# Six attention steps moved between the groups of the bias, the first two units in plain fp32 scores, a lag of four steps

## The chip, the cores and the metric

One core of a Trainium2 chip runs the whole program. The metric is the device time of one execution in microseconds (us). TensorE (PE) multiplies, VectorE (DVE), ScalarE (ACT) and GpSimd (POOL) work on tiles, and SyncE (SP) issues nearly all DMAs. PEld is the loading of weights into TensorE.

## The reference

Relative-position attention, whose output is the input of a three-way max MoE. B = 4, H = 8, S = 576, D = 64:

```python
scores = (q @ k.T) / sqrt(D)
psi = log1p(|i - j|) / log1p(max(i, 1))
bias = relu(psi[..., None] @ w1 + b1) @ w2          # (S, S, H), the same for every batch
attn = softmax(scores + bias)
x = (attn @ v) -> (2304, 512)
h = max(x @ m_w1, x @ m_w2, x @ m_w3)               # 512 -> 768
out = h @ m_w_out                                   # 768 -> 512
```

## The kernel before

The program has three stages.

**The bias** (`bias_stage`, L89). The 576 rows i are cut into 36 groups of 16. In iteration i the loop makes `hidden` of one group (four tiles `hid`, 128 x 304 to 576, by relu: three on DVE at L108 and one on ACT at L111, as a running balance `load` of the two engines decides), `product` of the group before (plain fp32 matmuls with `w2s` into a PSUM tile `bp`, L129) and `finish` of the one before that (`bp` scaled into `bs`, on ACT at L149 or on DVE at L152, and written by an SP DMA to `bias_d` in DRAM, L156). The groups 32 to 35 come first (`todo`, L132), since the small last row tile t = 4 (64 rows, `biasm`) needs them. `load_bias` (L162) reads the bias of one row tile t of a head pair back from `bias_d`, once all of its groups are written: the full tiles t = 0 to 3 are 576 KB each.

**Attention** (`Attention`, L182). There are 16 units (head pair, batch) of five row tiles t, 80 steps. A step n has a front end and a back end. In the front, `front` makes the scores `s` of both heads (one combined head for t = 4) as three fp32r products of high and low halves (L235, L244; the halves are made by `prep`, a cast on ACT at L212 and a subtraction on POOL at L213), `shift` adds the bias and takes the row minimum on DVE (L254), `expo` takes the exponential and its sum on ACT (L266, L270), and one step later `norm` takes the reciprocal on DVE (L276) and multiplies `e` by it on POOL (L279). In the back, LAG = 5 steps later, `flip` transposes `e` on PE into `tp` and `lp` (L298, L307) and ACT and DVE copy them to `et` (L389, L390, L392). Every 2 or 3 row tiles, five pairs of fp32 matmuls `pv` (L337) are queued; each step pops one to three of them. `split_x` (L345) splits the finished `pv` into `xhi` and `xlo`. The first five steps have no back end and run small `warm` matmuls on PE (L314).

**The MoE** (`moe`, L443): fp32r products of `xhi`, `xlo` with the weights' halves.

Every engine runs its instructions in the order of the program text; the order is written out by hand. PSUM tiles: `s` and `tp` have two buffers each, `lp` and `pv` one. In the bias stage `bp` takes all eight banks with four buffers; that pool is released before the attention's pool is opened (L542), so the first `s` comes after the last `bs`. `load_qk` brings the raw q and k of a unit (two buffers), `load_v` its v.

## Time and profile before

| | |
|---|---|
| median of 3 runs | 610.79 us (610.71 to 610.86) |
| profiled execution, span | 610.0 us |
| bias stage, first `hid` to the end of the last `bs` | 4.7 to 49.8 us |
| first matmul of the MoE | 310.7 us |
| PE busy | 600.2 us, 98% of the span |
| DVE, ACT, POOL busy | 368.1, 296.7, 171.0 us |

The profile is of one execution. A busy PE is not PE at its peak, since a matmul's end is modelled and a waiting one can look busy; so progress is read from the starts of steps, not from the busy share. In rows of the timeline that merge instructions, the time of one instruction is worked out from the start of the group and the start of what follows it.

### The profile page before, as it was taken

What the parts mean: (1) busy time and instruction counts of PE and PEld (TensorE: products, weight loads), DVE (VectorE), ACT (ScalarE), POOL (GpSimd) and SP (SyncE); (2) the same over time, 40 slices, a digit from 0 to 9 for tenths busy, and PEclk for the clock granted to TensorE, in tenths of its full rate; (3) what the DMA queues carried; (4) which work ended last, traced back from release to release, by engine and by line L of the source; (5) the groups of instructions that cost most, each with busy time, mean ns of one, the idle gap of its engine ahead of it and who ended that gap; (6) DMA issues with size and microseconds to landing.
All of it is one profiled execution on the core that took longest, in us unless ns stands there. A gap on an engine that the chain in (4) does not pass through costs nothing.

```text
span 610.0 us, 11550 instructions
## 1 busy us (share of the span) xinstructions
PE 600.2 (98%) x4288; PEld 464.0 (76%) x4288; DVE 368.1 (60%) x942; ACT 296.7 (49%) x791; POOL 171.0 (28%) x189
## 2 busy tenths in 40 slices
PE   8998899999999999999999999999999999999997
PEld 4456667776667767676678989889898898988886
DVE  7995776677777777776544746646464562233231
ACT  7997888888888888887510000000010001134432
POOL 2704766656676675574300000000000000000000
PEclk9999999999999999999999999999999999999999
DMA  5897435522462255200211212212122110011111
GB/s 170 245 332 257 144 93 144 156 72 70 148 172 61 62 165 163 62 16 18 55 35 35 70 34 70 69 35 72 40 65 66 40 64 1 1 53 70 52 70 69
DMA packets 48007, 55.16 MB, mean 90 GB/s; under 512 B 21968, under 2 KB 31568, under 8 KB 47952
## 3 DMA queue, kind: packets, MB, share of 16 engines
q1 hardware_dynamic: 47808, 54.14, 29.0%
q8 instruction: 34, 0.56, 0.4%
q10 hardware_dynamic: 144, 0.29, 0.2%
q14 instruction: 21, 0.17, 0.1%
HBM read 38.81 MB, written 15.61 MB: 89 GB/s over the span
## 4 chain that ended last, share of the span: by engine, by line
PE 90%; ACT 5%; DMA 2%; issue 2%; DVE 1%; SPq 0%; DVEq 0%
PE pv L337 14%; PE tp L298 12%; PE s L244 12%; PE h L483 8%; PE h L485 8%; PE h L484 8%; PE g L485 4%; PE g L483 4%; PE g L484 4%; PE o L508 4%; PE o L507 4%; PE o L509 4%; ACT bs L149 2%; ACT hid L111 2%; DMA bias<-bias_d 1%
## 5 line engine op out<-in xcount | busy, mean ns | idle before, releaser
L266 ACT ACTIVATE e<-sn,nm 128x576 f32<-128x576 f32 x144 | 110.9, 772 | 44.5 <-DVE nm L254 40.7
L279 POOL TENSOR_SCALAR e<-e,rc 128x576 f32<-128x576 f32 x144 | 105.8, 748 | 69.2 <-DVE rc L276 23.1
L254 DVE CUSTOM_DVE_ANT_0 sn<-s,bias 128x576 f32<-128x576 f32 x128 | 91.7, 754 | 42.6 <-PE s L244 36.8
L490 ACT COPY m<-h 128x512 f32<-128x512 f32 (+1 forms) x30 | 16.3, 544 | 206.2 <-PE h L485 180.9
L483 PE MATMUL h<-xhi,wh 128*128 128x512 f32 (+1 forms) x240 | 88.3, 368 | 0.0
L485 PE MATMUL h<-xhi,wl 128*128 128x512 f32 (+1 forms) x240 | 88.3, 368 | 0.0
L484 PE MATMUL h<-xlo,wh 128*128 128x512 f32 (+1 forms) x240 | 88.2, 368 | 0.0
L298 PEld LDWEIGHTS tp<-ident,e 128*128 128x128 f32 x576 | 61.5, 141 | 34.6 <-issue 29.4
L298 PE MATMUL tp<-ident,e 128*128 128x128 f32 x576 | 80.8, 280 | 0.9 <-ACT et L389 0.8
L337 PE MATMUL pv<-et,vt 128*64 128x256 f32 (+1 forms) x496 | 73.6, 417 | 0.0
L392 DVE COPY et<-tp 128x512 f32<-128x512 f32 x64 | 43.9, 686 | 26.3 <-PE tp L298 25.8
L244 PE MATMUL s<-kh,qh 64*128 64x288 f32 (+1 forms) x288 | 57.2, 343 | 2.3 <-DVE nm L254 1.4
L462 DVE TENSOR_TENSOR hl<-ht,hh 128x128 fp32r<-128x128 f32 x108 | 23.4, 286 | 44.9 <-ACT hh L461 44.9
L491 DVE TENSOR_TENSOR m<-h,m 128x512 f32<-128x512 f32 (+1 forms) x30 | 19.1, 638 | 50.9 <-ACT m L490 50.4
L483 PEld LDWEIGHTS h<-xhi,wh 128*128 128x128 f32 x240 | 45.1, 188 | 6.2 <-issue 0.5
L213 POOL TENSOR_TENSOR kl<-kr,kh 128x640 fp32r<-128x640 f32 x16 | 35.6, 2223 | 50.2 <-ACT kh L212 50.2
L484 PEld LDWEIGHTS h<-xlo,wh 128*128 128x128 f32 x240 | 45.0, 188 | 5.7
L485 PEld LDWEIGHTS h<-xhi,wl 128*128 128x128 f32 x240 | 45.0, 188 | 5.7
L389 ACT COPY et<-tp 128x512 f32<-128x512 f32 x80 | 45.8, 573 | 6.9 <-PE tp L298 6.9
L244 PE MATMUL s<-kl,qh 64*128 64x288 f32 (+1 forms) x288 | 48.6, 293 | 0.0
L244 PE MATMUL s<-kh,ql 64*128 64x288 f32 (+1 forms) x288 | 48.0, 290 | 0.0
L337 PEld LDWEIGHTS pv<-et,vt 128*64 128x64 f32 x496 | 30.3, 136 | 22.2 <-issue 9.8
(85 smaller groups left out, 1060.7 us busy)
## 6 DMA issues: line engine op xcount, KB each, us to landing
bias_d<-bs SPq DMA_DIRECT2D x36, 295.5 KB, 6.1
bias<-bias_d SPq DMA_DIRECT2D x16, 576.0 KB, 4.0
w<-in_moe_w_dram SPq DMA_DIRECT2D x18, 512.0 KB, 3.5
qr<-in_qd_dram SPq DMA_DIRECT2D x16, 320.0 KB, 3.2
kr<-in_kd_dram SPq DMA_DIRECT2D x16, 320.0 KB, 4.0
out_dram<-ot SPq DMA_DIRECT2D x17, 256.0 KB, 2.0
vt<-in_v_dram SPq DMA_DIRECT2D x32, 128.0 KB, 2.7
w64o<-in_moe_w_out_dram SPq DMA_DIRECT2D x6, 512.0 KB, 3.2
```

Source lines behind the costliest of these rows:

```text
L213: nc.gpsimd.tensor_tensor(out=lo, in0=r, in1=hi.bitcast(F32), op=ALU.subtract)
L244: nc.tensor.matmul(ss[h][:, x, 0:HALF], lhsT=u[q][p, r], rhs=u[k][p, c:c + HALF], start=(j == 0), stop=(j == 2))
L254: nc.vector.tensor_tensor_reduce(out=sn.rearrange("p (a b) -> p a b", a=2), in0=st["s"][h][:, :, 0:HALF], in1=bt.rearrange("p (a b) -> p a ...
L266: nc.scalar.activation(st["e"][:, S * h:S * h + S], sn, ACTF.Exp, scale=-1.0, bias=nm, accum_out=st["sm"][:, h:h + 1])
L279: nc.gpsimd.tensor_scalar(out=e, in0=e, scalar1=rc[:, h:h + 1], scalar2=1.0, op0=ALU.mult, op1=ALU.mult)
L298: nc.tensor.transpose(tp[:, 128 * c:128 * c + 128], e2[:, k0:k0 + 128], ident)
L337: nc.tensor.matmul(pv[p], lhsT=w, rhs=x, start=(c == 0), stop=(c == NTQ))
L389: nc.scalar.copy(*tps[0])
L392: nc.vector.tensor_copy(*tps[1])
L483: nc.tensor.matmul(o, lhsT=hi[:, r], rhs=x, start=(c == 0), stop=False)
L484: nc.tensor.matmul(o, lhsT=hi[:, r], rhs=y, start=False, stop=False)
L485: nc.tensor.matmul(o, lhsT=lo[:, r], rhs=x, start=False, stop=(c == KDM - 1))
```

## The change

- The scores `s` get a PSUM pool of their own that lives through the program; the bias products keep two `bp` buffers instead of four.
- Units 0 and 1 are never split by `prep`: their scores are one plain fp32 product of the raw q and k (L235). Their four casts on ACT and four subtractions on POOL go away.
- The fronts of units 0 and 1 run tile by tile (t = 4, 0, 1, 2, 3, each for unit 0 and unit 1). Six of these ten steps (t = 4, 0, 1) run in the bias stage: `front` in the iterations 12, 13, 21, 23, 29, 31, `shift` one iteration later, `expo` two and `norm` four iterations later. The balance `load` counts 770 ns a head for the shift on DVE and 970 ns a head for the exponential on ACT.
- The loads of the bias move: t = 4 from iteration 12 to 9, t = 0, 1, 2 from 19, 27, 35 to 17, 25, 33. Raw q and k get three buffers and come in iterations 0, 2 and 20, v of units 0 and 1 in iteration 14.
- After the bias stage the steps follow a written plan: the back ends start at once, four steps behind the fronts instead of five; two steps have no front; the `warm` matmuls are gone.

```diff
@@ -47,8 +47,10 @@
+    psum_s = ctx.enter_context(tc.tile_pool(name="psum_s", bufs=1, space=PSUM))
+
     def ps_s(name):
-        return psums[-1].tile([128, 2, 512], F32, tag="s", bufs=2, name=name)
+        return psum_s.tile([128, 2, 512], F32, tag="s", bufs=2, name=name)
...
-            bp = psums[-1].tile([128, 1024], F32, tag="bp", bufs=4, name=f"bp{g}")
+            bp = psums[-1].tile([128, 1024], F32, tag="bp", bufs=2, name=f"bp{g}")
...
+        nf = dict(zip(FIRST, range(len(FIRST))))
         for i in range(NG + 2):
             if i < NG:
                 hidden(todo[i])
             if 0 < i <= NG:
                 product(todo[i - 1])
+            if i in nf:
+                at.front(nf[i])
+            if i - 1 in nf:
+                n = nf[i - 1]
+                for h in range(at.heads(n)):
+                    at.shift(n, h)
+                    load["dve"] += 770
             if i > 1:
                 x = todo[i - 2]
                 finish(pool, k, load, x, late.pop(x))
+            if i - 2 in nf:
+                n = nf[i - 2]
+                for h in range(at.heads(n)):
+                    at.expo(n, h)
+                    load["act"] += 970
+            if i - 4 in nf:
+                at.norm(nf[i - 4])
...
-    sched = [(un, t) for un in range(len(units)) for t in range(NS)]
-
-    fronts = [sched[x] for x in (0, 1, 2, 4, 5, 3)] + sched[6:]
+    HEAD = [(un, t) for t in (4, 0, 1, 2, 3) for un in (0, 1)]
+    fronts = HEAD + [(un, t) for un in range(2, len(units)) for t in range(NS)]
+    sched = [(0, 0), (0, 1), (1, 0), (1, 1), (0, 2), (0, 4), (1, 2), (0, 3), (1, 4), (1, 3)]
+    sched = sched + fronts[len(HEAD):]
     NSTEP = len(sched)
-    LAG = NS
+    FIRST = (12, 13, 21, 23, 29, 31)
...
-            kr = pool.tile([128, S + LEFT], F32, tag="kr", bufs=2, name=f"kr{un}")
-            qr = pool.tile([128, S + LEFT], F32, tag="qr", bufs=2, name=f"qr{un}")
+            kr = pool.tile([128, S + LEFT], F32, tag="kr", bufs=3, name=f"kr{un}")
+            qr = pool.tile([128, S + LEFT], F32, tag="qr", bufs=3, name=f"qr{un}")
...
-            terms = (("qh", "kh"), ("qh", "kl"), ("ql", "kh"))
+            terms = (("qr", "kr"),) if "qr" in u else (("qh", "kh"), ("qh", "kl"), ("ql", "kh"))
...
-                st["e"] = pool.tile([128, 2 * S], F32, tag="e", bufs=NS + 2, name=f"e{n}")
+                nh = self.heads(n)
+                st["e"] = pool.tile([128, nh * S], F32, tag=f"e{nh}", bufs=7 if nh > 1 else 2, name=f"e{n}")
...
-        def warm(self, n):
-            w = psums[-1].tile([128, 128], F32, tag="l", bufs=1, name=f"warm{n}")
-            for _ in range(4):
-                nc.tensor.matmul(w, lhsT=ident, rhs=ident, start=True, stop=True)
...
-        def step(self, n, more=None):
-            m, f = n - 1, n - LAG
+        def step(self, n, f, pops, more=None):
             nh = 0
-            if n < NSTEP:
+            if n is not None:
                 un, t = fronts[n]
                 hp, b = units[un]
-                if t == 0 and un and un + 2 < len(units):
+                if t == 0 and 2 <= un < len(units) - 2:
                     self.load_qk(un + 2)
-                if t == 3 and un:
-                    self.load_v(un)
                 nh = self.heads(n)
                 self.front(n)
-            if n < NS:
-                self.warm(n)
-            for _ in range((1, 3, 2, 2, 2)[n % NS]):
-                if self.pvq and n >= LAG + TS + 1:
+                if (un, t) == HEAD[-1]:
+                    self.load_qk(3)
+            for _ in range(pops):
+                if self.pvq:
                     self.pvq.pop(0)()
-            back = 0 <= f < NSTEP
+            if n is not None and t == 4 and un > 1:
+                self.load_v(un)
...
+            for m in self.raw:
                 self.norm(m)
-            if n < NSTEP and un + 1 < len(units):
-                t0 = 1 if un == 1 else 0
+            self.raw = [] if n is None else [n]
+            if n is None:
+                un, t = (1, f - 2)
+            if 1 <= un < len(units) - 1 and (n is None or un > 1) and f < NSTEP:
...
+        def run(self, more):
+            lag = 4
+            first = len(FIRST)
+            plan = [(first, 0, 0), (first + 1, 1, 0), (None, 2, 2), (None, 3, 3), (first + 2, 4, 3), (first + 3, 5, 2)]
+            early = {6: 0, 7: 0, 8: 2, 9: 2, 10: 1}
+            for f in range(6, NSTEP):
+                n = f + lag if f + lag < NSTEP else None
+                plan.append((n, f, early.get(f, (3, 2, 2, 2, 1)[(f - 1) % NS])))
+            for n, f, pops in plan:
+                self.step(n, f, pops, more if f >= NSTEP - 60 and (n is None or n % NS >= 2) else None)
+            while self.pvq:
+                self.pvq.pop(0)()
+            self.split_x()
...
-            for g, _ in enumerate(bias_stage(bp)):
+            for g, _ in enumerate(bias_stage(bp, at)):
                 if g == 0:
                     at.load_qk(0)
+                if g == 2:
+                    at.load_qk(1)
+                if g == 9:
+                    load_bias(0, NTQ)
+                if g in (17, 25, 33):
+                    load_bias(0, (g - 17) // 8)
+                if g == 14:
                     at.load_v(0)
-                    first = at.prep(0)
-                if g in (5, 8):
-                    next(first)
-                if g == 16:
-                    at.load_qk(1)
-
-                if g == 12:
-                    load_bias(0, NTQ)
-                if g in (19, 27, 35):
-                    load_bias(0, (g - 19) // 8)
+                    at.load_v(1)
+                if g == 20:
+                    at.load_qk(2)
             load_bias(0, NTQ - 1)
-            at.load_qk(2)
...
-        while n < NSTEP + LAG:
-            at.step(n, w0 if n >= NSTEP - 60 and n % NS >= 2 else None)
-            n += 1
-        while at.pvq:
-            at.pvq.pop(0)()
-        at.split_x()
+        at.run(w0)
```

## Rows read from the trace of the kernel before

**Rows 1.** The page, busy time and share of the span of PE:
```profile
PE 600.2 (98%) x4288; PEld 464.0 (76%) x4288; DVE 368.1 (60%) x942; ACT 296.7 (49%) x791; POOL 171.0 (28%) x189
```

**Rows 2.** Stretches: length, busy us of each engine, granted PE clock, DMA share, GB/s:
```profile
40.00:50.00 10.00, 8.84 (x130) 4.23 (x121) 8.51 (x22) 8.79 (x15) 0.00 (x0) 1.00 1.01 349
50.00:60.00 10.00, 9.19 (x78) 7.72 (x80) 5.42 (x17) 7.02 (x18) 5.55 (x6) 1.00 0.66 209
60.00:70.00 10.00, 8.75 (x78) 6.69 (x75) 6.80 (x20) 7.78 (x22) 5.77 (x9) 1.00 0.69 217
100.00:110.00 10.00, 10.00 (x87) 6.96 (x86) 6.87 (x20) 7.11 (x21) 5.91 (x7) 1.00 0.75 208
```

**Rows 3.** Timeline of DVE and ACT in the bias stage: start, us, instruction, [idle before]:
```profile
4.71 18.93 DVE L108 TENSOR_SCALAR hid<-sm,bp 128x528 f32<-128x528 f32 x48
...
32.47 6.66 DVE L108 TENSOR_SCALAR hid<-sm,bp 128x304 f32<-128x304 f32 x21
...
47.96 0.83 DVE L152 TENSOR_SCALAR bs<-bp,sm 128x591 f32<-128x591 f32 x1 [0.28 <-issue]
...
49.09 0.75 ACT L149 ACTIVATE bs<-bp,sm 128x591 f32<-128x591 f32 x1 [1.06 <-PE bp L129]
```

**Rows 4.** Groups by line, 0 to 50 us: busy, mean ns | idle before, releaser:
```profile
L152 DVE TENSOR_SCALAR bs<-bp,sm 128x591 f32<-128x591 f32 x4 | 3.3, 827 | 0.5 <-issue 0.3 <-ACT hid L111 0.2
...
L149 ACT ACTIVATE bs<-bp,sm 128x591 f32<-128x591 f32 x32 | 24.4, 761 | 2.9 <-PE bp L129 2.9
```

**Rows 5.** Timeline of one step's shift (DVE), exponentials (ACT), copies of a back end (ACT):
```profile
51.09 0.76 DVE L254 CUSTOM_DVE_ANT_0 sn<-s,bias 128x576 f32<-128x576 f32 x1 [2.30 <-DMA bias_d<-bs]
...
52.46 0.08 DVE L254 DVE_READ_ACCUMULATOR2_ANT nm<- 128x1 f32 x1
...
51.90 0.78 ACT L266 ACTIVATE e<-sn,nm 128x576 f32<-128x576 f32 x1 [2.06 <-DVE nm L254]
...
53.67 0.71 ACT L212 CAST kh<-kr 128x640 fp32r<-128x640 f32 x1
...
128.10 0.58 ACT L389 COPY et<-tp 128x512 f32<-128x512 f32 x1
...
128.73 0.78 ACT L266 ACTIVATE e<-sn,nm 128x576 f32<-128x576 f32 x1
```

**Rows 6.** Chain that ended last, PE's pieces: start, us, what:
```profile
27.38 5.25 PE bp L129 x80
...
118.09 0.99 PE s L244 x12
119.08 1.01 PE pv L337 x8
120.10 1.02 PE tp L298 x8
...
133.78 0.98 PE s L244 x9
```

**Rows 7.** POOL beside DVE: timeline of POOL, then DVE's groups by form:
```profile
12.77 12.29 POOL L213 TENSOR_TENSOR kl<-kr,kh 128x640 fp32r<-128x640 f32 x1 [10.71 <-ACT kh L212]
25.02 1.66 POOL L213 TENSOR_TENSOR ql<-qr,qh 128x640 fp32r<-128x640 f32 x1
...
129.80 1.48 POOL L279 TENSOR_SCALAR e<-e,rc 128x576 f32<-128x576 f32 x2
...
L108 DVE TENSOR_SCALAR hid<-sm,bp 128x384 f32<-128x384 f32 x6 | 3.7, 666 | 0.0
...
L108 DVE TENSOR_SCALAR hid<-sm,bp 128x400 f32<-128x400 f32 x6 | 2.2, 422 | 0.0
```

**Rows 8.** DMA issues at 22.6, 31.3 and 58.5 us: KB, us to landing:
```profile
biasm<-bias_d SPq DMA_DIRECT2D x1, 144.0 KB, 3.4
...
bias<-bias_d SPq DMA_DIRECT2D x1, 576.0 KB, 7.8
...
bias<-bias_d SPq DMA_DIRECT2D x1, 576.0 KB, 5.3
```

**Rows 9.** Timeline of PE: front of step n = 8, first matmul of the MoE:
```profile
71.00 0.40 PE L244 MATMUL s<-kh,qh 64*128 64x288 f32 x2
...
310.70 0.50 PE L483 MATMUL h<-xhi,wh 128*128 128x512 f32 x1
```

More of the change, by code (lines that the diff above doesn't have):

```diff
@@ L186, in __init__ @@
             self.st = {}
-            self.et = {}
+            self.ets = {}
+            self.left = {}
+            self.raw = []
             self.pvq = []
@@ L244, in front @@
                         nc.tensor.matmul(ss[h][:, x, 0:HALF], lhsT=u[q][p, r], rhs=u[k][p, c:c + HALF],
-                                         start=(j == 0), stop=(j == 2))
+                                         start=(j == 0), stop=(j == len(terms) - 1))
             self.st[n] = dict(s=ss)
@@ L286, in flip @@
             w = 128 * TS if g == 0 else S - 128 * TS
-            if t in (0, TS):
+            if (un, g) not in self.ets:
                 et = pool.tile([128, (2 * NTQ + 1) * (S - 128 * TS)], F32, tag="et", bufs=2, name=f"et{un}_{g}")
-                self.et = (et[:, 0:2 * NTQ * w].rearrange("p (c h q) -> p c h q", c=NTQ, h=2),
-                           et[:, 2 * NTQ * w:(2 * NTQ + 1) * w])
-            ea, el = self.et
+                self.ets[un, g] = (et[:, 0:2 * NTQ * w].rearrange("p (c h q) -> p c h q", c=NTQ, h=2),
+                                   et[:, 2 * NTQ * w:(2 * NTQ + 1) * w])
+                self.left[un, g] = TS if g == 0 else NS - TS
+            ea, el = self.ets[un, g]
             c0 = 128 * t - 128 * TS * g
@@ L340, in pair @@
                 return run
-            self.wait = True
             self.pvq.extend(pair(c) for c in range(NTQ + 1))
@@ L375, in step @@
                 next(more, None)
-            if n < NSTEP and b == B - 1 and hp + 1 < HP:
+            if n is not None and b == B - 1 and hp + 1 < HP:
                 load_bias(hp + 1, t)
-            if 0 <= m < NSTEP:
+            for m in self.raw:
                 self.norm(m)
-            if n < NSTEP and un + 1 < len(units):
-                t0 = 1 if un == 1 else 0
+            self.raw = [] if n is None else [n]
+            if n is None:
+                un, t = (1, f - 2)
+            if 1 <= un < len(units) - 1 and (n is None or un > 1) and f < NSTEP:
+                t0 = 1 if un == 2 else 0
                 if t == t0:
@@ L386, in step @@
             self.split_x()
-            if back:
+            if f is not None:
                 tps, left = self.flip(f)
@@ L392, in step @@
                     nc.vector.tensor_copy(*tps[1])
-            if back:
                 un, t = sched[f]
@@ L396, in step @@
                 w = 128 * TS if g == 0 else S - 128 * TS
-                if t in (TS - 1, NS - 1):
-                    self.queue_pv(un, 128 * TS * g, w, *self.et)
+                self.left[un, g] -= 1
+                if self.left[un, g] == 0:
+                    self.queue_pv(un, 128 * TS * g, w, *self.ets[un, g])
+        def run(self, more):
[11 more added lines that the diff above has]
+            self.split_x()
     def convert(pool, src, hi, lo, name, split=None):
```

5 lines of the change are left out of this document (2 added, 3 removed).

## The prediction, made before the changed kernel was run

> **What bounds the kernel now.** I read the page first: PE is busy 98% of the span [rows 1], which only says that most of the program is PE's. So I looked for the stretches where it is not, with the stretches by engine [rows 2]. From 100 us on PE is full and a unit takes 133.78 - 118.09 = 15.7 us, start to start [rows 6]; nothing there can be gained but PE work. The bias stage is another matter: DVE and ACT are nearly full, DMA is saturated at its end [rows 2], and the timeline shows DVE going from 4.71 to 48.79 with almost no gap [rows 3], 0.5 us of idle time in all against 2.9 us on ACT [rows 4]. DVE bounds that stage, ACT closely behind; its last `bs` ends at 49.84. Then comes a refill, 50 to 71 us: steps without back ends, bias loads that are waited for, two engines half used [rows 2]. From the front of step 8 at 71.00 PE runs without a break to the MoE at 310.70, 239.7 us later [rows 9].
>
> So the change pays through the refill: between 49.84 and 71.00 the old kernel does 8 fronts and 3 back ends, some 12 us of PE work in 21 us. It is paid for in the bias stage, on DVE, which has nothing to spare. The whole question is the size of that bill.
>
> **The bias stage, part by part.** Start: 44.08 us of DVE from 4.71 to 48.79.
>
> Taken away. The casts of unit 0 leave ACT and its two subtractions leave POOL. The latter matter: the first sat on POOL from 12.77 for 12.29 us, and while both were finishing, DVE's 384-wide `hid` slowed: six average 666 ns where the 400-wide take 422 [rows 7]. At 0.41 each these six should take 2.5 us and took 4.0, so DVE lost 1.5. With that and the 0.5 of idle time gone, 42.1 us of DVE work remain.
>
> Added. A two-head shift takes 52.46 - 51.09 + 0.08 = 1.45, a single one 0.76 [rows 5]: 4 x 1.45 + 2 x 0.76 = 7.3. Six reciprocals have no row here; at the size of the accumulator's read, 0.08 [rows 5], 0.5. The running balance, worked out by its formulas, gives DVE 4 `bs` before (as the trace shows [rows 4]) and 4 after, and moves four `hid` from ACT to DVE: at 0.32 to 0.39 (6.66/21 and 18.93/48 [rows 3]) 1.4. DVE: 42.1 + 7.3 + 0.5 + 1.4 = 51.3, from 4.7 to 56.0. The last `bs` waits for the last product, 1.05 us of PE (5.25 for five groups [rows 6]) with one `bs` between: 0.4, so 56.4 without any other wait.
>
> ACT gets 4 x 1.77 [rows 5] and 2 x about 1.05 for the exponentials, loses 1.2 of casts and 2.1 of `hid`: 42.2 busy becomes 48.1, done by about 53. It stays behind DVE. PE has 36 x 1.05 + some 6.5 for the fronts, 44 in 52 us: room enough, and two `bp` buffers suffice, since a product needs only the `bs` two groups before it.
>
> Waits that are new, each in DVE's queue with the `hid` of the next groups behind it, and through them PE and ACT:
> - t = 4: three loads issued after iteration 9's write land 3.4 us after issue [rows 8], some 5 us after that `bs`; DVE's four iterations take 4.5. Wait 0.4.
> - t = 0: behind iteration 17's write (0.6 to issue) the 576 KB take 5.3 in a calm queue and 7.8 in a saturated one [rows 8]; the v loads and the slower groups leave the queue calmer than before, so 5.3. DVE reaches the shift after 15 `hid` of 0.31, 4.8 us. Wait 1.1, at 7.8 it would be 3.6.
> - t = 1 has seven iterations' worth of time: 0.2.
> - Each front is emitted an iteration ahead of its shift: product and front, 1.05 + 1.1, against two iterations' `hid`, 2.1. Nothing.
> - POOL now multiplies ten heads by reciprocals here, 0.74 each [rows 7]. The row at 12.77 says that POOL waits out an unbroken run of `hid` and gets in when DVE does something else; the shifts, the DVE `bs` and the wait for t = 0 are such places and hold all but about one of the ten. I take 0.7; the ends are 0 and 7.4.
>
> Here the Trainium skill speaks against the change (SBUF — State Buffer, "Who interferes with whom"): a DVE `tensor_scalar` in a two-port mode and a GpSimd instruction share one port pair, and whichever issues first holds it for its whole duration while the other blocks. The slow `hid` agree with it. By that rule alone all ten multiplications could hold DVE up, and the stage would end 6.7 us later than in my sum.
>
> Sum: 56.4 + 0.4 + 1.1 + 0.2 + 0.7 = 58.8, 9.0 later than before. That is B.
>
> **The refill.** Plain fp32 scores: no row shows them. Nearest are plain fp32 `pv` pairs, 1.01 for two pairs of 256 columns, so 1.13 for two of 288; the fp32r front takes 0.99 [rows 6]. If the two heads did not run together on PE's row halves, 2.3. The fp32r heads do, and fp32 column halves do: 1.13.
>
> The first front of the plan runs on PE before B. Its shift starts at about B + 0.2 (bias t = 2, loaded four iterations earlier), its exponentials 0.8 later, and take 1.77; the copies of the first back end 0.63 [rows 5]: B + 3.4. The second front waits for the `s` buffers till B + 1.7, ends at 2.8, its exponentials begin at 3.7, end at 5.4; copies to B + 6.1. Only then can the first `pv` run. ACT bounds these 6.1 us, PE stands about half of them.
>
> From there compare with the old step 8. Still to do are the same 72 fronts and 160 `pv` pops, one more transposed step (1.02 and 0.1 for `lp` [rows 6]) and 0.25 for two plain fronts: 1.4. The steps five to eight back ends on have few or no pops: PE has 2.1 us, ACT 1.77 + 0.63 and a cast of 0.6 in two of them. Followed through, PE loses 0.4, 0.6 and 1.2 there: 2.2. The t = 3 bias lands by B + 11 (write, then 5.3), its front's successor needs it at B + 12: nothing. After that the lag of four is enough: with two heads the copies of a step end 4.4 to 5 us after its front starts, and the next transposes come at 5 or later, so the unit stays at 15.7.
>
> MoE start: 58.8 + 6.1 + 1.4 + 2.2 + 239.7 = 308.2 instead of 310.7. The MoE is untouched. Span 610.0 - 2.5 = 607.5; the median stands 0.8 above the profiled span, so **608.3 us**. The granted clock is 1.00 throughout [rows 2], its 2.4 GHz level; the `warm` matmuls fill waits and cost nothing. PE's longest new wait is under 2 us; no row here shows the lower level, so its price has no bound and sits in the tail.
>
> **The rivals.**
> 1. **DVE isn't held up and the refill is dense.** For: neither the waits (2.4) nor the 2.2 of ACT-bound steps has a row; against: the copies follow the exponentials on ACT by the program's order. 608.3 - 4.6 = 603.7. Chance 0.18.
> 2. **POOL holds DVE.** The multiplications start in the gap of a reciprocal and each stops the next `hid`. For: 1.5 us lost to two POOL instructions [rows 7]; against: the first of these waited 11 us without harm. Each head exposed beyond the one counted costs 0.74; from five on (3.7) the kernel is slower than before by over 0.2%; eight give 608.3 + 5.9 = 614.2, six 612.7. I take **612.7**. Chance 0.16.
> 3. **The bias loads come late.** At 7.8 instead of 5.3 the wait for t = 0 grows by 2.5: 610.8, no change. For: DMA share 1.01 before [rows 2]; against: the qk loads no longer fall there. Chance 0.16.
> 4. **Plain fp32 scores cost double**, so that the change doesn't do what it says: 1.1 more for each of four fronts in the bias stage, where shifts wait for them, and four behind it: 608.3 + 8.8 = 617.1. Chance 0.05.
>
> **How the numbers follow.** The forecast (its own range 606.3 to 610.3) has 0.45. A measurement of this kernel can tell about 0.2%, 1.2 us, from no change. Faster by more: rival 1 and most of the forecast, 0.18 + 0.39 = 0.57. Within: 0.06 + 0.13 = 0.19 with part of rival 3, and 0.02 of rival 2: 0.21. Slower: 0.22. The range of 8 in 10 reaches from rival 1 to just above rival 2: 603.7 to 613.
>
> **What would show each step.** In the changed profile: the last `bs` at 58.8 (56.4 without waits); the 384-wide `hid` back near 0.41, or many `hid` over 0.6 if rival 2 holds; shifts waiting for `bias` at iteration 22 for 1 us; a plain front of 1.1 us; the first `pv` 6 us after the last `bs`; 15.7 a unit from the third unit on; the MoE at 308. The prediction is wrong if the stage ends past 61 or before 57, or if the unit's period moves: 0.2 us there is 2.8 in the whole.

## The result and the profile after

The changed kernel takes 618.36 us (617.57 to 619.48) against 610.83 for the kernel before: ratio 1.0122, 95% interval 1.0108 to 1.0137. The forecast of 608.3 was wrong, in sign too, and its range (up to 613.0) did not hold the time.

The page of the changed kernel: span, then busy time, share and instructions of each engine.

```profile
span 616.1 us, 11319 instructions
...
PE 601.3 (98%) x4212; PEld 455.8 (74%) x4212; DVE 373.4 (61%) x946; ACT 294.4 (48%) x783; POOL 156.9 (25%) x185
```

As in [rows 1], that tells next to nothing: 1.1 us more of PE in a span 6.1 us longer. Again the stretches say where to look (length, busy us of PE, PEld, DVE, ACT, POOL, granted PE clock, DMA share, GB/s):

```profile
30.00:40.00 10.00, 7.81 (x104) 3.55 (x104) 5.61 (x17) 6.47 (x11) 1.05 (x1) 1.00 0.79 237
40.00:50.00 10.00, 9.06 (x72) 3.95 (x72) 9.88 (x29) 6.57 (x15) 1.88 (x2) 0.66 0.79 267
60.00:70.00 10.00, 7.91 (x84) 4.36 (x77) 8.19 (x18) 5.96 (x15) 3.55 (x4) 1.00 0.80 241
70.00:80.00 10.00, 8.43 (x67) 5.49 (x65) 5.26 (x14) 6.09 (x16) 5.99 (x6) 1.00 0.36 104
```

DVE, almost without a gap before [rows 3], is busy for only 5.6 of the ten microseconds from 30, and the stage still runs when the old one had been over for 10 us. DVE's timeline names what it waits for (start, us, instruction, how many, [idle before <- releaser]):

```profile
23.67 0.76 DVE L274 CUSTOM_DVE_ANT_0 sn<-s,biasm 128x576 f32<-128x576 f32 x1 [2.12 <-DMA biasm<-bias_d]
...
30.66 4.95 DVE L110 TENSOR_SCALAR hid<-sm,bp 128x352 f32<-128x352 f32 x15
...
40.12 0.76 DVE L274 CUSTOM_DVE_ANT_0 sn<-s,bias 128x576 f32<-128x576 f32 x1 [4.51 <-DMA bias<-bias_d]
...
65.90 0.83 DVE L169 TENSOR_SCALAR bs<-bp,sm 128x591 f32<-128x591 f32 x1 [1.26 <-PE bp L131]
```

Two bias loads come late (2.1 and 4.5 us of an empty DVE), and the last group output waits 1.3 for its product; it ends at 66.73, where the forecast had 58.8. PE behind it, the same view: the first `pv`, a plain front of two heads with what follows it, the start of the MoE.

```profile
72.62 1.15 PE L354 MATMUL pv<-et,vt 128*64 128x256 f32 x8 [1.57 <-ACT et L406]
...
77.42 1.24 PE L264 MATMUL s<-kr,qr 64*128 64x288 f32 x8
78.59 1.51 PE L354 MATMUL pv<-et,vt 128*64 128x256 f32 x12
...
316.80 0.50 PE L514 MATMUL h<-xhi,wh 128*128 128x512 f32 x1
```

So first `pv` 5.9 us after the stage, the MoE 244.2 us after that, at 316.8 instead of 310.7 [rows 9]. **From the first `pv` on almost nothing is lost**: a unit takes 15.70 us as before, the MoE stage 299.3 in both kernels, and the 244.2 are 0.9 more than forecast. The rest was lost in the bias stage.

### The profile page after: what moved, and what is told of

Its sections match the earlier page's. It is cut to its first block, busy times and chain, and to the rows that moved or that the text cites. A ratio compares the mean times of both kernels' runs of the same rounds, so it can differ in the third digit from the quotient of the medians.

```text
span 616.1 us, 11319 instructions
## 1 busy us (share of the span) xinstructions
PE 601.3 (98%) x4212; PEld 455.8 (74%) x4212; DVE 373.4 (61%) x946; ACT 294.4 (48%) x783; POOL 156.9 (25%) x185
## 4 chain that ended last, share of the span: by engine, by line
PE 86%; DVE 5%; ACT 4%; DMA 3%; issue 1%; SPq 0%; DVEq 0%; ACTq 0%
PE pv L354 14%; PE tp L320 11%; PE s L264 11%; PE h L514 8%; PE h L515 8%; PE h L516 8%; PE g L515 4%; PE g L516 4%; PE g L514 4%; PE o L539 4%; PE o L538 4%; PE o L540 4%; DVE hid L110 4%; ACT e L287 2%; DMA bias_d<-bs 1%
## 5 line engine op out<-in xcount | busy, mean ns | idle before, releaser
L300 POOL TENSOR_SCALAR e<-e,rc 128x576 f32<-128x576 f32 x144 | 108.3, 765 | 125.4 <-DVE rc L297 118.7
L131 PE MATMUL bp<-hid,w2s 128*32 128x79 f32 (+51 forms) x640 | 44.5, 412 | 5.0 <-DVE hid L110 2.3
L264 PE MATMUL s<-kh,qh 64*128 64x288 f32 (+1 forms) x252 | 48.9, 344 | 0.0
L110 DVE TENSOR_SCALAR hid<-sm,bp 128x480 f32<-128x480 f32 (+17 forms) x112 | 44.6, 475 | 0.0
L514 PE MATMUL g<-xhi,wh 128*128 128x512 f32 (+1 forms) x120 | 44.0, 367 | 0.0
```

Source lines behind the costliest of these rows:

```text
L110: nc.vector.tensor_scalar(out=h[:, 0:n], in0=wl[:, 0:n], scalar1=k["bp"][:, m:m + 1], scalar2=0.0, op0=ALU.add, op1=ALU.max)
L131: nc.tensor.matmul(bp[32 * c:32 * c + 32, o:o + w], lhsT=w2s, rhs=src, start=True, stop=True)
L264: nc.tensor.matmul(ss[h][:, x, 0:HALF], lhsT=u[q][p, r], rhs=u[k][p, c:c + HALF], start=(j == 0), stop=(j == len(terms) - 1))
L300: nc.gpsimd.tensor_scalar(out=e, in0=e, scalar1=rc[:, h:h + 1], scalar2=1.0, op0=ALU.mult, op1=ALU.mult)
L514: nc.tensor.matmul(o, lhsT=hi[:, r], rhs=x, start=(c == 0), stop=False)
```

## The experiments

All edits are to the changed kernel unless said otherwise. "Stage end" is the end of the last `bs` on either engine. In the profiles of twelve of the fourteen edited versions of the changed kernel the MoE starts 244.0 to 244.3 us after the first `pv`; the time of that `pv` is therefore the number to compare. The two exceptions are named.

**1. The v loads (`e1_v_late`).** SP's issues in the changed kernel (start, us, what): three of the eight v loads, the group writes behind them, and the t = 0 bias load.

```profile
25.27 0.98 SPq L243 DMA_DIRECT2D vt<-in_v_dram  x1
...
29.58 1.47 SPq L243 DMA_DIRECT2D vt<-in_v_dram  x1
31.10 0.52 SPq L244 DMA_DIRECT2D vl<-in_v_dram  x1
31.71 1.85 SPq L173 DMA_DIRECT2D bias_d<-bs  x3
33.62 0.60 SPq L181 DMA_DIRECT2D bias<-bias_d  x1
```

Eight issues of 0.5 to 1.5 us keep SP from 25.27 to 31.62; the group writes and the bias load queue behind them. The edit:

```diff
-                if g == 14:
+                if g == 26:
                     at.load_v(0)
                     at.load_v(1)
```

> The changed kernel with the loads of v of units 0 and 1 moved from iteration 14 to 26, nothing else. Theory A (the time went into DVE waits and POOL's hold on DVE in the bias stage): the eight issues took SP from 25.3 to 31.6 us, so the t = 0 bias was issued at 33.6 and DVE waited 4.5 us for it. Without them it is issued near 28.5 and the wait is 0 to 1 us; the last bs ends 3.5 to 4.5 us earlier (about 62.5) and the kernel takes 614 to 615. The granted clock should then not fall at 41 us. Theory B (the slow clock from 41 to 48 us and the two bp buffers, not the wait, make the stage long): the end of the stage follows the clock, so it also comes earlier, but by the products' share and with DVE still idle elsewhere. Theory C (DVE is simply full, the wait only fills room that another wait would take): under 1 us gained.

Measured: 615.18 us, ratio 1.0066 (1.0042 to 1.0090), just above theory A's range. In its profile SP issues the t = 0 load at 30.10 instead of 33.62, and DVE's shift no longer waits for the load but for the scores:

```profile
35.44 0.76 DVE L274 CUSTOM_DVE_ANT_0 sn<-s,bias 128x576 f32<-128x576 f32 x1 [1.12 <-PE s L264]
```

DVE reaches this shift at 34.32 (35.44 less the wait), 4.2 us after the issue; in the changed kernel it does so at 35.61, 2.0 after the issue. So the issue came 2.2 us late there, and the landing took 6.4 where I had 5.3: with the 1.1 that I had given, that is the wait of 4.5. The other runs agree: with the v loads in iteration 14 this wait was 2.80 to 4.33 us and the load landed 6.3 to 6.5 after its issue (`e2_norm_after`, `e3_qk_early`, `e7_warm`); with them later and the t = 0 steps in their place it was 1.34 to 2.18, with landings of 5.0 to 5.8 (`e5_v_norm`, `e6_v_norm_warm`, `e10_fronts4`, `e11_fronts6`). Stage end 62.06 (from 66.73), first `pv` 68.31 (from 72.62); of these 4.3 us 3.4 are this shift, and 1.7 the t = 4 wait (0.45 for 2.12), ahead of which nothing was changed; the shift behind the stage waits 0.7 for its bias instead. In the medians 3.2 us of the 7.5 lost go with the place of the v loads. The executions run from 613.6 to 617.2 and mostly follow the granted clock, 1.000 to 0.994 over the whole program; the third group below takes that up.

**2. The q and k loads of unit 1 (`e3_qk_early`).** The wait of 2.1 us for the t = 4 load I put down to `load_qk(1)`, 640 KB issued ahead of it.

```diff
                     at.load_qk(0)
-                if g == 2:
                     at.load_qk(1)
```

> The changed kernel with q and k of unit 1 loaded in iteration 0 instead of 2. Theory A: those 640 KB were issued at 9.5 us in front of the writes of the first groups; the write of group 35 took 6.4 us to land, SP held the t = 4 bias back to 19.2 and DVE waited 2.1 us for it. With the load in the calm before, the t = 4 bias comes about 2 us earlier, the wait falls to 0 to 0.5, the stage ends 1 to 2 us earlier, 616.5 to 617.5 us. Rival (the wait is not on the chain, since the t = 0 bias is what holds DVE later): the wait for t = 0 grows by what was won here and the kernel stays at 618.

Measured: 617.84, 1.0097 (1.0071 to 1.0123). The t = 4 wait stayed, 2.52, but for another reason. The last of the three t = 4 loads, 16 KB, as SP issues it in the changed kernel, then in `e3_qk_early`:

```profile
21.10 0.60 SPq L185 DMA_DIRECT2D biasm<-bias_d  x1
...
19.08 0.60 SPq L185 DMA_DIRECT2D biasm<-bias_d  x1
```

It lands 2.5 us after the start of its issue in the first and 4.8 us in the second, in both just before the shift. So the wait of the changed kernel was a late issue (SP had waited 0.8 us for a group's write to land, and the second load took 1.26 to issue), that of `e3_qk_early` a slow landing. The early issue can't be credited to the edit: `e1_v_late`, `e2_norm_after` and `e5_v_norm`, in which nothing ahead of this load was changed, issue it at 18.8 to 19.2 too, with landings of 2.9, 3.9 and 2.9 and waits of 0.45, 1.56 and 0.58 at that shift. The cause that I named is not borne out; what makes the issue or the landing late in one execution and not in the other is open.

**3. POOL's multiplications (`e2_norm_after`, `e5_v_norm`).** POOL in the changed kernel (start, us, what, [idle <- releaser]); the last row is a pair beside which DVE is nearly idle:

```profile
46.14 1.88 POOL L300 TENSOR_SCALAR e<-e,rc 128x576 f32<-128x576 f32 x2 [14.26 <-DVE rc L297]
50.11 1.93 POOL L300 TENSOR_SCALAR e<-e,rc 128x576 f32<-128x576 f32 x2 [2.10 <-DVE rc L297]
60.30 2.08 POOL L300 TENSOR_SCALAR e<-e,rc 128x576 f32<-128x576 f32 x2 [8.25 <-DVE rc L297]
64.74 1.47 POOL L300 TENSOR_SCALAR e<-e,rc 128x576 f32<-128x576 f32 x2 [2.36 <-DVE rc L297]
```

Each pair starts 0.25 us or less after the start of its reciprocal (45.89, 49.87, 60.05) in the midst of `hid`, and does not wait for the end of the run of `hid`, as the first row of [rows 7] had made me think. The edit takes the six norms out of the loop and puts them behind the last `hidden`; `e5_v_norm` is that and the edit of `e1_v_late`.

```diff
-            if i - 4 in nf:
-                at.norm(nf[i - 4])
+            if i == NG - 1:
+                for n in (2, 4, 3, 5, 0, 1):
+                    at.norm(n)
```

> The changed kernel with the six norms of the bias stage made after the last hidden (iteration 35) instead of four iterations after each front. Theory A: POOL's multiplications beside DVE's hid cost about 0.42 us a head, 3.5 us in all (hid 43.8 us in sum against 40.1 by the widths); without them the hid return to the old times, the last bs ends 2.5 to 3.5 us earlier, the refill loses at most 1 us, and the kernel takes 615 to 616.5. The waits for the bias of t = 4 and t = 0 grow by what DVE arrives earlier (up to 0.8). Rival, as forecast: POOL holds DVE for only one of ten, 0.7 us, kernel 617.5 to 618.4.

> Both of the earlier edits on the changed kernel: v of units 0 and 1 loaded in iteration 26, norms after the last hidden. Theory A (waits and POOL's hold on DVE): the two add up, the last bs at 58.5 to 60 us, MoE starts 6 to 8 us earlier than in the changed kernel if PE's granted clock stays at 1.00 in the refill; 610.5 to 612.5 us. Theory E (formed from the runs: the granted clock falls where PE waits in the refill, since the warm matmuls are gone): the times come in two groups, 610.5 to 612 at clock 1.00 and 613 to 615.5 at 0.99, by executions of the same kernel.

Measured: 616.24, 1.0082 (1.0067 to 1.0097), and 615.71, 1.0073 (1.0054 to 1.0093). DVE's `hid`, all 112, and by form the 496-wide (busy us, mean ns | idle before): the changed kernel first,

```profile
L110 DVE TENSOR_SCALAR hid<-sm,bp 128x480 f32<-128x480 f32 (+17 forms) x112 | 44.6, 475 | 0.0
...
L110 DVE TENSOR_SCALAR hid<-sm,bp 128x496 f32<-128x496 f32 x7 | 3.8, 602 | 0.0
```

then `e2_norm_after`:

```profile
L110 DVE TENSOR_SCALAR hid<-sm,bp 128x480 f32<-128x480 f32 (+17 forms) x112 | 40.9, 445 | 0.0
...
L110 DVE TENSOR_SCALAR hid<-sm,bp 128x496 f32<-128x496 f32 x7 | 2.9, 477 | 0.0
```

The same 112 tiles cost 44.6 - 40.9 = **3.7 us** more with POOL among them: eight heads before the last `hid`, 0.46 each. (`e1_v_late` and `e5_v_norm`, which differ in the same edit, have the same 44.6 and 40.9.) POOL's pairs pay too, 1.9 to 2.1 instead of 1.47. `e2_norm_after` ends its stage at 62.74, 4.0 earlier, and has its first `pv` at 68.74; `e5_v_norm` ends it at 59.44, 0.6 from the forecast's 58.8. But the times gain 2.1 and 2.7 us only (neither theory had 615.71 for `e5_v_norm`), and `e5_v_norm` is no better than `e1_v_late`, which still has POOL's hold. The first shift behind the stage of `e5_v_norm`, and its stretches, show why:

```profile
62.51 0.76 DVE L275 CUSTOM_DVE_ANT_0 sn<-s,bias 128x576 f32<-128x576 f32 x1 [3.07 <-DMA bias<-bias_d]
```

```profile
60.00:62.00 2.00, 0.84 (x8) 0.60 (x6) 0.00 (x0) 0.00 (x0) 2.00 (x4) 1.00 1.02 394
62.00:64.00 2.00, 0.67 (x2) 0.50 (x2) 1.49 (x5) 0.69 (x2) 2.00 (x3) 0.74 0.66 257
64.00:66.00 2.00, 2.00 (x8) 1.30 (x6) 0.90 (x2) 1.78 (x7) 0.76 (x2) 0.50 0.07 28
...
70.00:72.00 2.00, 2.00 (x11) 1.12 (x8) 0.00 (x0) 0.00 (x0) 2.00 (x2) 0.50 0.03 8
```

Now that the stage ends early, the first step behind it waits 3.07 us for the t = 2 bias: its shift starts at 62.51, against 62.73 in `e1_v_late`, so this wait alone takes back nearly all of the 2.6 us by which the stage ends earlier, and even the one execution of `e5_v_norm` at granted clock 1.00 takes 614.30 (those of `e1_v_late` 613.61, 613.99 and 615.18). Moreover PE does little from 60 to 63, and from there until 73 its granted clock is 0.50, the 1.2 GHz level: the first pair of `pv` takes 2.04 us instead of 1.15. In `e2_norm_after` the clock fell at 69 to 72 and again at 90 to 93, and there the MoE starts 247.3 us after the first `pv`, 3.1 more than elsewhere.

**4. The clock (`e4_no_fronts`, `e6_v_norm_warm`, `e7_warm`).** The kernel before has `warm` matmuls in its first steps; the change drops them. `e4_no_fronts` moves no front into the bias stage; `e6_v_norm_warm` is `e5_v_norm`, and `e7_warm` the changed kernel, with four plain fp32 128 x 128 matmuls ahead of two steps.

```diff
-    FIRST = (12, 13, 21, 23, 29, 31)
+    FIRST = ()
...
-            first = len(FIRST)
...
+            first = 6
+            plan = [(i, None, 0) for i in range(first)]
```

```diff
+            if f in (2, 8):
+                self.warm(f)
             for _ in range(pops):
```

> The changed kernel with no front in the bias stage: all ten steps of units 0 and 1 follow it, the first six without a back end; plain fp32 scores, lag four, early bias loads and two bp buffers stay. Theory A: the bias stage shrinks to DVE's own work without POOL beside it, last bs at 47.5 to 48.5 us (49.8 before the change); six steps bound by ACT at 1.8 take 9 to 11 us, the first pv comes 6 us later, at 63 to 65 (72.6 in the changed kernel), and the kernel takes 608 to 611, so that moving the fronts into the bias stage is the whole loss. Theory B (two bp buffers make the stage long): last bs not before 52. Rival D (plain fp32 scores and the lag of four cost the steady part): first pv at 63 to 65, yet 614 or more.

> The run before with four small fp32 matmuls put back at two places where PE waited for ScalarE's copies (ahead of the first pv and ahead of the pv of the eighth back end, waits of 1.6 and 1.2 us). Theory E: the granted clock stays at 1.00 in the refill in all executions, and the times are one group, 610.5 to 612.5. If the clock doesn't matter: the same times as without them, or up to 1 us more.

> The changed kernel with these small matmuls alone. Theory E: the clock still falls at 41 us in the bias stage (PE waits there for the t = 0 bias), where DVE bounds and it costs nothing, and no more in the refill; the kernel takes 616 to 618, 0 to 2 less than the changed one. If the fall in the bias stage costs: no change.

Measured: `e4_no_fronts` 616.91, 1.0085 (1.0055 to 1.0114). Its stage ends at 49.26, where the old one did, and yet it is slow, and none of its three theories has the first `pv` at 69.96. One stretch of its refill, and the same of `e9_fronts0` (below), which is the same order of work with later v loads and with warm matmuls in the steps that have no back end:

```profile
60.00:62.00 2.00, 2.00 (x6) 0.91 (x6) 1.33 (x5) 1.29 (x3) 0.29 (x1) 0.50 0.04 17
```

```profile
60.00:62.00 2.00, 2.00 (x15) 1.43 (x12) 1.42 (x5) 1.52 (x4) 1.36 (x2) 1.00 0.92 267
```

Six matmuls at clock 0.50 in the time of fifteen at 1.00 (eight of these are `warm` ones, of about the same length). The executions of `e4_no_fronts` go with the mean granted clock: 612.25 and 612.9 at 1.00, 615.2 to 618.1 at 0.992 to 0.994, 619.37 at 0.989, 620.21 at 0.986. `e9_fronts0` holds 1.00 in all, 614.06 to 614.18, but it is slower than `e4_no_fronts` at 1.00: the `warm` matmuls have a price, which the sixth group takes up. That it is they that hold the clock is likely and not isolated, since the v loads differ too. `e6_v_norm_warm`, 614.98, 1.0070 (1.0049 to 1.0091), holds it in the refill (first `pv` 68.32, the MoE 244.05 later) but met a longer wait for the t = 0 bias, 2.18, so that its stage ended at 62.33, the t = 2 bias was not waited for, and PE met no wait like that of `e5_v_norm`. So it does not test what the `warm` matmuls do there, and its gain over `e5_v_norm` is not beyond the intervals. `e7_warm`, 618.81, 1.0122 (1.0099 to 1.0144), gains nothing: in the change as given the refill kept its clock anyway (that of `e7_warm` fell in the bias stage, at 47 to 51 and at the last products, 64 to 68). There the clock falls in the bias stage. The changed kernel:

```profile
38.00:40.00 2.00, 0.83 (x16) 0.17 (x8) 0.00 (x0) 0.65 (x1) 0.00 (x0) 1.00 1.03 401
...
42.00:44.00 2.00, 2.00 (x10) 0.95 (x12) 2.00 (x7) 1.88 (x5) 0.00 (x0) 0.50 1.02 389
```

PE had waited from 38.8 to 40.9 with DVE for the t = 0 bias; from 41.5 until 48.4 it runs at the lower level. It costs the stage nothing there: DVE is busy for all of the 2.00 us and shows no wait again until its last `bs`.

**5. Plain scores alone (`e8_before_plain`).** The kernel before, with plain fp32 scores for units 0 and 1 and thus without their casts and subtractions.

```diff
-            terms = (("qh", "kh"), ("qh", "kl"), ("ql", "kh"))
+            terms = (("qr", "kr"),) if "qr" in u else (("qh", "kh"), ("qh", "kl"), ("ql", "kh"))
...
-                    first = at.prep(0)
-                if g in (5, 8):
-                    next(first)
```

> One part alone on the kernel before: units 0 and 1 in plain fp32 scores, so that their four casts and four subtractions are gone (four buffers for raw q and k); order, lag of five, four bp buffers, loads and warm matmuls as before. Theory A: without the subtraction on POOL the three 384-wide hid take 0.41 each instead of 0.66, 1.70 and 0.41, and the bias stage ends 1 to 2 us earlier (last bs at 48 to 49); plain scores cost 0.18 a front in the refill, which ACT hides. MoE 1 to 2.5 us earlier, 608.5 to 610. Rival: the refill waits for the t = 3 bias, whose last write sits in the DMA queue, and nothing moves: 610.5 to 611.

Measured: 610.75, 1.0001 (0.9987 to 1.0014). The `hid` that POOL's subtractions had held up [rows 7] are back at their widths: DVE's eighteen behind 24 us, the kernel before first, then `e8_before_plain`:

```profile
24.63 7.18 DVE L108 TENSOR_SCALAR hid<-sm,bp 128x384 f32<-128x384 f32 x18
...
24.29 5.65 DVE L108 TENSOR_SCALAR hid<-sm,bp 128x384 f32<-128x384 f32 x18
```

DVE's last `bs` comes at 46.08 instead of 47.96 [rows 3]. The time does not move beyond the interval and lies in the rival's range: the first step then waits 2.48 us for its scores and the third 2.12 for its bias. So the 1.5 us that I credited are real in the stage and bring nothing measurable alone; what the change gains it has to gain by the moved fronts.

**6. How much a moved front is worth (`e9_fronts0`, `e12_fronts2`, `e10_fronts4`, `e11_fronts6`).** Common to the four: norms behind the last `hidden`, `load_v(0)` at group 36 and `load_v(1)` behind the last bias load, warm matmuls in the steps without a back end and in the two of `e6_v_norm_warm`. They differ in the fronts that are moved: none, (12, 13), (12, 13, 21, 23), all six; and with them in the steps without a back end behind the stage, each with its `warm` matmuls: six, four, two, none.

```diff
-                if g == 14:
+                if g == 36:
                     at.load_v(0)
-                    at.load_v(1)
...
             load_bias(0, NTQ - 1)
+            at.load_v(1)
...
+            if f is None or f in (2, 8):
+                self.warm(f)
```

> A series of four kernels that differ in one number, the fronts made in the bias stage. Common to them: the changed kernel with norms after the last hidden, v of unit 0 loaded in iteration 36 and v of unit 1 behind the last bias load, and small fp32 matmuls on PE in the steps that have no back end, ahead of the first pv and of the pv of the eighth back end. This one: no front in the bias stage. Theory E (the clock falls where PE waits, and warm matmuls hold it): against the earlier kernel without fronts, whose executions went from 612.3 at clock 1.00 to 620.2 at 0.986, all are near 1.00 and 609.5 to 612. Theory F (a front in the bias stage costs there what it saves later, since DVE is full): this is the fastest of the four or equal to them. Theory A alone (only waits and POOL's hold made the moved fronts dear): slower than the others, 612 to 613.

> As the series, with the two single-head fronts (t = 4) in iterations 12 and 13. Theory F: two shifts of 0.76 and up to 0.5 of hid moved to DVE in the bias stage, two single-head steps of 1.1 less on ScalarE behind it: the same as without fronts within 1 us, plus the wait for the t = 4 bias (0.5 to 2). Theory A alone: 1 to 2 us faster than without fronts.

> As the series, with four fronts (t = 4 and t = 0 of both units) in iterations 12, 13, 21, 23. Theory F: DVE's stage 1.5 + 2.9 + about 1 longer than without fronts, the refill 2.2 + 3.6 shorter, and the waits for the t = 4 and t = 0 bias on top, 1 to 3: 0 to 3 us slower than without fronts. Theory A alone: 2 to 4 us faster than without fronts.

> As the series, with all six fronts where the change puts them. Theory F: last bs at 58.5 to 60, 11 us later than without fronts, the refill 9 to 10 shorter; 612 to 614, 1 to 3 us slower than without fronts. Theory A alone (with the waits and POOL's hold gone the change pays as forecast): 607 to 609.5.

Measured, all at granted clocks of 0.999 or 1.000 in the profiles:

| fronts moved | stage end | first `pv` | time, us | ratio (95%) |
|---|---|---|---|---|
| 0 | 48.96 | 68.89 | 614.15 | 1.0052 (1.0037 to 1.0067) |
| 2 | 52.17 | 68.17 | 613.53 | 1.0042 (1.0028 to 1.0057) |
| 4 | 55.75 | 66.77 | 612.57 | 1.0031 (1.0021 to 1.0041) |
| 6 | 59.96 | 67.09 | 612.20 | 1.0019 (1.0006 to 1.0031) |

By the table, a moved front lengthens the stage by 1.8 us and shortens what lies between it and the first `pv` by 2.1: 0.3 us each net on average, 2.0 for six. By it, too, the expectation that they make the kernel slower fell, and so did those of 609.5 or less with six and of 609.5 to 612 without any.

But the series does not isolate the fronts, since with each one a block of `warm` matmuls goes too, and a block takes 1.05 to 1.16 us of PE ahead of the next scores. `e4_no_fronts` has neither moved fronts nor blocks. The shift of its fifth step behind the stage, before its clock falls at 58, and the same shift of `e9_fronts0`:

```profile
56.84 0.76 DVE L274 CUSTOM_DVE_ANT_0 sn<-s,bias 128x576 f32<-128x576 f32 x1 [0.78 <-PE s L264]
...
58.28 0.76 DVE L276 CUSTOM_DVE_ANT_0 sn<-s,bias 128x576 f32<-128x576 f32 x1 [1.20 <-PE s L266]
```

`e9_fronts0` is 1.4 us behind there, though its stage ended 0.3 us earlier, so the blocks can account for 1.7 of the 2.0 us. The two executions of `e4_no_fronts` at clock 1.00 fit that: 612.25 and 612.9, against 612.20 with six fronts. So a moved front is worth something between nothing and 0.3 us net, and the runs do not narrow it further, since `e4_no_fronts` has other v loads and its profile is of an execution whose clock fell. The expectation that a front costs in the stage what it saves behind it is not refuted.

With all six the first `pv` is no earlier than with four. Two waits stand on DVE in that profile (the last row is PE's):

```profile
35.63 0.76 DVE L276 CUSTOM_DVE_ANT_0 sn<-s,bias 128x576 f32<-128x576 f32 x1 [2.03 <-DMA bias<-bias_d]
...
59.13 0.83 DVE L171 TENSOR_SCALAR bs<-bp,sm 128x591 f32<-128x591 f32 x1 [0.95 <-PE bp L131]
...
56.63 2.43 PE L131 MATMUL bp<-hid,w2s 128*32 128x495 f32 x32 [0.96 <-ACT bs L168]
```

The second comes from the two `bp` buffers: PE's last two products wait 0.96 for ScalarE's `bs`, which stands behind the last two exponentials.

**7. The waits that were left (`e13_t0_later`, `e14_t1_early`, `e15_t2_early`, and `e16_before_t2_early`).** One after the other on `e11_fronts6`: the t = 0 steps two groups later; the t = 1 steps and their load two groups earlier; the t = 2 load three groups earlier. `e16_before_t2_early` makes only the last of these moves, in the kernel before (35 to 30).

```diff
-    FIRST = (12, 13, 21, 23, 29, 31)
+    FIRST = (13, 14, 23, 25, 29, 31)     # e13
+    FIRST = (13, 14, 23, 25, 27, 29)     # e14, e15
...
-                if g in (17, 25, 33):
+                if g in (17, 23, 33):        # e14: t = 0, 1, 2
+                if g in (17, 23, 30):        # e15
```

> As e11, with the six early steps' scores at groups 13, 14, 23, 25, 29, 31 instead of 12, 13, 21, 23, 29, 31: the t=0 bias load is issued where it was, and the shift that waits for it stands two groups (some 2.6 us) later. Theory W (the waits are what is missing): the 2.0 us wait at the first t=0 shift falls under 0.3 us, VectorE's last group output ends 1 to 2 us earlier, and the time falls from 612.2 to 610.3 to 611.3. Rival Q (the stage was not bounded by that wait, since work behind it fills what follows, and the refill takes back what is gained): the wait goes and the time stays within 0.5 us of 612.2.

> As e13, with the t=1 steps' scores at groups 27 and 29 instead of 29 and 31 and the t=1 bias load issued after group 23 instead of 25: the last two exponentials leave ScalarE before the last two group outputs, so the last two products no longer wait 1.0 us for their accumulator. Theory W: another 0.5 to 1.0 us off e13, to 609.5 to 610.7, at or under the kernel before (610.9). Rival Q: no change against e13. A third way: the t=1 load now lands after its shift wants it, a wait of 1 us or more moves there, and the time is that of e13 or above.

> As e14, with the t=2 bias load issued after group 30 instead of 33 (the last group that it reads is written by iteration 29). Theory W (each of these waits stands on the path): the 2.9 us wait at the first shift behind the stage falls to about 1.2, where the last group output and the scores' buffers are next, and the time falls from 611.05 to about 609.5 (608.8 to 610.2), under the kernel before by 0.1 to 0.3%. Rival Q (ScalarE, with 1.77 us of exponentials and 0.63 of copies a step, bounds the refill whatever the first shift does): 610.7 to 611.4.

> The kernel before, with its t=2 bias load issued after group 30 instead of 35, nothing else. If that load is on its path too (its third step waits 1.9 us for it at 56.97): 609.5 to 610.3 instead of 610.5. If it isn't, because ScalarE and the lag of five steps fill what is gained or because the load then delays the loads before it: 610.3 to 611.0.

| kernel | stage end | first `pv` | MoE | time, us | ratio (95%) |
|---|---|---|---|---|---|
| `e13_t0_later` | 60.09 | 67.20 | 311.31 | 611.63 | 1.0013 (1.0003 to 1.0023) |
| `e14_t1_early` | 58.41 | 65.76 | 309.83 | 611.05 | 1.0004 (0.9995 to 1.0014) |
| `e15_t2_early` | 59.16 | 65.14 | 309.21 | 610.36 | 0.9989 (0.9980 to 0.9998) |
| `e16_before_t2_early` | 49.96 | 71.71 | 310.44 | 614.48 | 1.0059 (1.0046 to 1.0073) |

In `e13_t0_later` the t = 0 wait went, 2.03 to 0.47, and a shift of t = 1 waits 1.6 for its scores instead: neither theory alone. `e14_t1_early` has a median 0.6 lower and shows the next wait, which `e15_t2_early` halves:

```profile
60.17 0.76 DVE L276 CUSTOM_DVE_ANT_0 sn<-s,bias 128x576 f32<-128x576 f32 x1 [2.93 <-DMA bias<-bias_d]
```

```profile
59.56 0.76 DVE L276 CUSTOM_DVE_ANT_0 sn<-s,bias 128x576 f32<-128x576 f32 x1 [1.44 <-PE s L266]
...
65.14 1.15 PE L361 MATMUL pv<-et,vt 128*64 128x256 f32 x8 [0.68 <-ACT et L415]
...
309.21 0.49 PE L524 MATMUL h<-xhi,wh 128*128 128x512 f32 x1
```

The three edits were aimed at waits of 2.0, 1.0 and 2.9 us. The first `pv` came 67.09 - 65.14 = 1.95 us earlier, and the ratio fell by 0.0030, 1.8 us; only the three together are beyond the intervals, not each by itself. So both theories were half right: the waits stood on the path, and a third of them came back, since the scores were next late, 0.5 to 1.6 us behind. **The result is a version 0.1% faster than the kernel before** (the interval ends at 0.9998), by less than the 0.2% that I called no change, and by the medians 8.0 us faster than the change as given.

`e16_before_t2_early` says that the load is no gift to the old kernel: the wait that it removes (1.88 at 56.97, now 0.95 for the scores) leaves the time at 611.53 in the one execution at granted clock 1.00, and the other five, at 0.993 to 0.997, take 613.8 to 615.0, above both expected ranges. That the clock falls in them because a filled wait has become an empty one is likely from group 4, but the profile is of the execution at 1.00, so it is not shown.

## Why the prediction was wrong, step by step

The forecast put the MoE's start at 308.2; it came at 316.8, 8.6 later. The stage end has 7.9 of these (66.7 for 58.8), the refill -0.2 and the rest 0.9. In the stage, the waits for t = 0 and t = 4, POOL's hold and the tail came out 3.4, 1.7, 3.0 and 0.9 above the forecast; the wait for t = 1 (0.2) did not show, and DVE's own work was 0.9 shorter. Two rivals, POOL and the late loads, came true together; the chances had taken them one at a time.

- **What bounds the kernel**: right. The stage is DVE's, all that matters happens before the first `pv`, and a unit stays at 15.7.
- **DVE's own work**, 56.0: right. `e5_v_norm`, with POOL away and the v loads late, ends at 59.44 with waits of 0.6, 0.4, 1.3, 0.6 and 0.95 in front of its shifts and its last `bs`, 55.6 without them. The "Nothing" for shifts that wait for their scores was too little, though it is hidden behind the late loads here: 0.45, 0.49 and 1.12 in `e1_v_late`.
- **The wait for t = 0**, 1.1 forecast, 4.5 measured. The step that failed is "the v loads and the slower groups leave the queue calmer than before, so 5.3". I reckoned the landing of the load and did not walk SP's issues: the v loads, moved to iteration 14 and doubled to eight issues, made the issue itself 2.2 us late, and the landing took 1.1 more. The rival with the late loads had the right place and a price of 2.5 instead of 3.4.
- **The wait for t = 4**, 0.4 forecast, 2.1 measured here and 0.4 to 2.5 in other runs with the same steps. The landing was no longer than forecast here (2.5 us for the last part); the issue was 1.9 to 2.3 us later than in `e1_v_late`, `e2_norm_after` and `e5_v_norm`. The forecast had no term for that, and its cause is open.
- **POOL holding DVE**, 0.7 forecast, 3.7 measured. The step that failed is "POOL waits out an unbroken run of `hid` and gets in when DVE does something else; the shifts, the DVE `bs` and the wait ... hold all but about one of the ten". POOL starts 0.25 us after the start of the reciprocal that releases it, in the midst of `hid`; that reciprocal seems to be gap enough. The rival said so, with a price of 0.74 a head; it is 0.46.
  The Trainium skill (SBUF — State Buffer, "Who interferes with whom") has whichever of a two-port `tensor_scalar` of DVE and a GpSimd instruction issues first hold the shared ports for its whole duration, while the other blocks; with POOL first each time, eight heads would cost DVE an estimated 5.9 us. The trace agrees with the conflict and not with that size: 3.7 on DVE, and POOL's pairs lengthened by 0.4 to 0.6, so both slow down.
- **The tail**, 0.4 forecast, 1.3 measured: "two `bp` buffers suffice" holds for the body of the stage, where DVE shows no wait for a product here, and fails at its end, where a `bs` stands behind others' work on its engine and PE's last product waits for it (0.63 us for DVE's `bs` here, 0.96 for ScalarE's in `e11_fronts6`). How much of the tail four buffers would take away was not tried.
- **The refill**, 6.1 forecast, 5.9 here, 6.0 in `e15_t2_early`: right, and ScalarE bounds it as followed through. A plain front takes 78.59 - 77.42 = 1.17 for 1.13 forecast, so the rival of doubled scores is out.
- **After the first `pv`**, 243.3 forecast, 244.0 to 244.3 in all changed versions whose clock holds there: 0.8 too little, of which the runs don't say what.
- **Outside the span**, 0.8 forecast. In every run the time stands about 1.8 above the span of the same execution, with the old kernel too (610.53 on 608.7). The 0.8 was a median of 610.79 against the span of another execution, 610.0, that was itself 1 us longer (611.72). So the old kernel's typical MoE start is 610.8 - 1.8 - 299.3 = 309.7 rather than 310.7, and 1.0 us of the forecast's gain of 2.5 was never there.
- **The clock**: "the `warm` matmuls fill waits and cost nothing" priced taking them out at nothing. In the change as given that did no harm, since its clock fell only under DVE's cover; in `e5_v_norm` and `e2_norm_after`, which end the stage earlier, the lower clock took back 1.8 and 3.1 us behind the first `pv` alone (245.9 and 247.3 for 244.1). "PE's longest new wait is under 2 us" was nearly right (2.12 here) and no safeguard: the clock fell behind that wait, and in `e2_norm_after` behind shorter ones.

These tell what even the stage as forecast would have brought. With 244.1 us from the first `pv` to the MoE and 6.0 from the stage end to the first `pv`, the change is level with the old kernel (309.7) when its stage ends at 309.7 - 250.1 = 59.6. The forecast's own 58.8 was 0.8 us short of that: no change that a measurement can tell. `e15_t2_early`, at 59.16, shows just this.

## What to carry to other kernels

Before a transfer is moved past other issues on its queue, write the queue's issues down with their times: the late load here was above all a late issue, behind eight small ones. Work moved into a stage that one engine bounds is paid for twice, by its own time there and by each wait that it brings into that engine's queue, and the gain is only the difference between stretching one stage and shortening the next (for a front here at most 0.3 us of 2.1, and perhaps nothing). In a series that is to price one thing, see that nothing else changes with it: the `warm` matmuls that went with each moved front can make up most of what the fronts seemed to bring. Compare a sum made on a profiled execution with the time of that execution, not with the median of others.

## What the hardware showed that I had not expected

- PE's granted clock fell to 0.50 behind a wait of 2.12 us in the changed kernel (from 41.5), of 2.49 in `e5_v_norm` (from 63), of 1.67 and of 1.27 in `e2_norm_after` (from 69 and from 90), and in `e4_no_fronts` (from 58) with no wait above 0.39 ahead of its last fronts; behind a wait of 1.57 in the changed kernel (at 72.6) it stayed at 1.00. So the length of one wait does not tell. It stayed down for 3 to 10 us with PE at work again. The executions of one and the same kernel, `e4_no_fronts`, spread over 8 us with it (612.25 at 1.00 to 620.21 at 0.986). With `warm` matmuls in the waits, and later v loads, all of `e9_fronts0` held 1.00, at the price told in the sixth group.
- POOL's 576-wide multiplication beside DVE's `hid` takes 0.46 us of DVE for 0.74 of its own and becomes a third longer itself. A subtraction in the same place is in the trace for 12.29 us [rows 7], one with DVE less busy (at 73.9 in the changed kernel) for 1.54; what decides between the two is open.
- A small DMA of 16 KB (the last t = 4 load) takes 0.6 us or more of SP to issue and lands 2.3 to 4.8 us after its issue, about as long as one nine times its size [rows 8].
